# One transfer of an attention decode kernel written as 8 runs of 16 rows, and three small loads merged into others

## The chip, the cores and the metric

The kernel runs on one core of one Trainium2 chip. The metric is the device time of one execution in microseconds (us), as the median of a few runs. Beside it stands one profiled execution, whose span (first to last recorded instruction) is what the trace shows.

## The reference, cut to what matters

Two sequences (batch 2) decode one token each: a conditioned layer norm, attention over a cache of 4,096 positions in 32 heads of 128, a second conditioned layer norm and a two-layer feed-forward with Mish.

```
mod = (silu(c) @ w_mod).reshape(2, 6, 1, 512)        # sa, ca, ga, sb, cb, gb
h = layernorm(x) * (1 + ca) + sa
x = x + ga * (softmax(q(h) @ k_cache) @ v_cache) @ wo # 32 heads, 4096 positions
h = layernorm(x) * (1 + cb) + sb
x = x + gb * (mish(h @ w1 + b1) @ w2)
```

All of it is float32. The two caches hold 268 MB, the weights the rest of the 297 MB that are read; each byte is used for two tokens only.

## The kernel before, in words

All input is packed on the host into 42 loads, each one tile of SBUF with 128 rows (partitions). A head's `k` or `v` is 8,192 columns (32 KB a row). Tiles come from two pools: `one` (one buffer of 12,288 columns) and `two` (two buffers of 16,384 columns), in the rotation two, one, two. So three loads are on the chip at a time, and `used()` issues load n as soon as all that load n-3 held has been consumed. SyncE (SP) issues every load, in the order of the list that `stream()` writes, on one queue; the transfers of a load are cut at the widths that stand beside its keys. ScalarE (ACT) issues three small loads at the start on a queue of its own: the two rows of `head` (`cq`, `xq`, 8 partitions each) and `b1c` (128 partitions of 48 B).

Load 0 holds three parts of `w_mod` (`m012`) and the first two blocks of `wq`. TensorE (PE) makes the first modulation and the first `q` from it. Then for each head VectorE (DVE) multiplies `k` by `q` (L316) and sums over the head's 128 elements (L319), ACT takes the exponentials (L339), and PE multiplies them with `v` (L365), some heads behind.

The last three loads set the tail. The first holds the last block of `wo`, `m4`, and the last head's `v` in three transfers; the second `m3` and `w1` in three; the third `m5` and `w2` in five, whose last two are 512 columns each (2 KB a row, 256 KB in all). When the last `v` has been used, a chain of small steps follows on all engines: `x2`, its mean and variance (`centred`), the modulations by `m4` and `m3`, the hidden layer `w1ps` (L521), Mish, and the output `yps` (L561), which uses `w2` block by block. `busy(n)` puts matmuls on PE whose result is not used. SP at last stores `y` (L571).

Of the kernel before, what the change touches and what calls it, by code (L numbers as in the profile page):

```python
# [8 lines left out]
F32 = mybir.dt.float32  # L9
# [4 lines left out]
P = 128  # L14
WIDTHS = (384, 384, 352, 256)
CHUNKS = [(g, j) for j in range(3) for g in range(4) if WIDTHS[g] > P * j]
HEADS = 32
HC = 4
BIG = 8192
W = 2048  # L20
SIZES = {
    "k": BIG, "v": BIG, "wq": W, "wo": W, "m012": 3 * W, "m3": W, "m4": W, "m5": W,
    "w1": 4 * sum(WIDTHS), "w2": 512 * len(CHUNKS),
}
AHEAD = (14, 22)


def stream():

    behind, pieces = {}, [("k", 0)]
    for h in range(1, HEADS):
        pieces.append(("k", h))
        if h not in AHEAD:
            behind[h] = len(behind)
            pieces.append(("v", behind[h]))
    left = list(range(len(behind), HEADS))
    pieces += [("v", h) for h in left[:-1]]

    extra = {}
    for c in range(2, HEADS // HC):
        at = (pieces.index(("k", HC * c)) - 1) // 5 * 5
        extra[at] = [("wq", c), ("wo", c - 2)]
    extra[60] = [("wo", HEADS // HC - 2)]
    loads = [[([("m012", 0), ("wq", 0), ("wq", 1)], (3 * W, 2 * W))]]
    n = 0
    while n < len(pieces):
        m = 1 if n % 5 == 0 else 2
        keys = pieces[n : n + m]  # L50
        if keys[0] == ("v", left[0]) and m == 2:
            loads.append([([key], (BIG,)) for key in keys])
        else:
            keys = keys + (extra.pop(n, []) if m == 1 else [])
            loads.append([(keys, (sum(SIZES[kind] for kind, _ in keys),))])
        n += m
    assert not extra and len(loads) % 3 == 0
    last = HEADS - 1
    loads += [
        [([("wo", HEADS // HC - 1), ("m4", 0)], (2 * W,)), ([("v", last)], (BIG // 2, BIG // 4, BIG // 4))],  # L60
        [([("m3", 0), ("w1", 0)], (W, 2 * sum(WIDTHS), 2 * sum(WIDTHS)))],
        [([("m5", 0), ("w2", 0)], (W, 6 * 512, 3 * 512, 512, 512))],
    ]
    return loads, behind, left
# [3 lines left out]
def kernel(  # L68
# [1 line left out]
    tc: tile.TileContext,  # L70
    loads: list,
    head: bass.AP,
    b1c: bass.AP,
    behind: dict,
    left: list,
    out: bass.AP,
# [9 lines left out]
    nc = tc.nc  # L86
    ctx.enter_context(tc.manual_schedule())
    B = 2
    DH = 128
    D = 512  # L90
    G = D // P
    R = P // G
    TB = R // B
    H = HEADS
    NS = BIG // (B * DH)
    NJ = 3
    EPS = 1e-5
    SCALE = DH ** -0.5
    NCH = len(CHUNKS)

    const = ctx.enter_context(tc.tile_pool(name="const", bufs=1))
    work = ctx.enter_context(tc.tile_pool(name="work", bufs=2))
# [18 lines left out]
    def take(t, keys):  # L121
        lo = 0
        for kind, n in keys:
            part = t[:, lo : lo + SIZES[kind]]
            lo += SIZES[kind]
            if kind in "kv":
                (k_t if kind == "k" else v_t)[n] = part.rearrange("p (b j d) -> p b j d", b=B, d=DH)
            elif kind in ("wq", "wo"):
                (wq_t if kind == "wq" else wo_t)[n] = part.rearrange("p (k n) -> p k n", k=G)
            else:  # L130
                w_t[kind] = part.rearrange("p (k n) -> p k n", k=NCH if kind == "w2" else G)

    w_t = {}
    done = set()

    def load(n):

        t = room(n)
        lo = 0
        for keys, srcs in loads[n]:  # L140
            take(t[:, lo:], keys)
            for src in srcs:
                nc.sync.dma_start(out=t[:, lo : lo + src.shape[-1]], in_=src)  # L143
                lo += src.shape[-1]

    loaded = 0

    def used(*keys):

        nonlocal loaded  # L150
        done.update(keys)
        while loaded < len(loads) and (
            loaded < 3 or all(key in done for keys, _ in loads[loaded - 3] for key in keys)
        ):
            load(loaded)
            loaded += 1
# [1 line left out]
    used()  # L158


    cq = work.tile([P, P], F32, tag="xn", name="cq", bufs=1)
    xq = const.tile([P, P], F32, name="xq")
    for t, src in ((cq, head[0]), (xq, head[1])):
        nc.gpsimd.memset(t, 0.0)
        nc.scalar.dma_start(out=t[::TB, :], in_=src)
    bias = const.tile([P, NCH + 1], F32, name="bias")
    nc.scalar.dma_start(out=bias, in_=b1c)
    nc.scalar.preload_act_table_set("natural_log_exp_and_others")
    ident = const.tile([P, P], F32, name="ident")
    make_identity(nc, ident)  # L170
# [3 lines left out]
        out=fold, in_=ident.rearrange("p (g r) -> p r g", g=G), axis=AX.X, op=ALU.add  # L174
# [3 lines left out]
        out=mean_w, in0=fold[:, None, :].to_broadcast([P, G, R]), scalar1=1.0 / D, scalar2=None, op0=ALU.mult  # L178
# [55 lines left out]
    def modulation(name, n, t, ps=None, ks=range(G)):  # L234


        if ps is None:
            ps = wide_ps(f"modps{name}")[:, : n * P].rearrange("p (m n) -> p m n", m=n)
        for k in ks:
            for g in range(G):  # L240
                nc.tensor.matmul(  # L241
                    ps[R * g : R * (g + 1)],
                    lhsT=ct[:, k, :],
                    rhs=t[:, k, :].rearrange("p (m n) -> p m n", m=n)[:, :, P * g : P * (g + 1)],
                    start=(k == 0),
                    stop=(k == G - 1),
                )
        return ps
# [8 lines left out]
    xn = work.tile([P, P], F32, tag="xn", name="xn", bufs=1)  # L257
    xc, var, rs = centred(xq, "a")
# [1 line left out]
    nc.vector.tensor_scalar(out=xn, in0=xc, scalar1=y0, scalar2=y1, op0=ALU.mult, op1=ALU.mult)  # L260

    fps = psum.tile([P, 512], F32, tag="att2", name="fps", bufs=1)[:, : NJ * G * B]
    nc.tensor.matmul(fps, lhsT=ident, rhs=bias[:, :, None].to_broadcast([P, NJ * G, B]), start=True, stop=False, skip_group_check=True)  # L263

    ps = modulation("0", 3, w_t["m012"])
    hq = const.tile([P, P], F32, name="hq")
# [1 line left out]
    nc.vector.tensor_tensor(out=hq, in0=ps[:, 0, :], in1=hq, op=ALU.add)  # L268
    mod = {}

    def keep(m, ps):
        mod[m] = const.tile([P, P], F32, name=f"mod{m}")
        nc.scalar.copy(mod[m], ps)

    keep(2, ps[:, 2, :])
    hps = columns(hq, "hps")
    hc = const.tile([P, G, B], F32, name="hc")
    nc.vector.tensor_copy(hc, hps)  # L278
# [14 lines left out]
    def busy(n):  # L293

        for lo in range(0, n, 2):
            cols = P * min(2, n - lo)
            nc.tensor.matmul(ov[1][:, :cols], lhsT=ident, rhs=e_t[0][0].rearrange("p c m -> p (c m)")[:, :cols], start=True, stop=True)
# [130 lines left out]

    project_q(0)
    project_q(1)  # L430
    used(("m012", 0), ("wq", 0), ("wq", 1))
    for h in range(H):
        products(h)
        if h:
# [61 lines left out]
    def add_x(total):  # L496
        nc.vector.scalar_tensor_tensor(x2, xg, 1.0, xq, op0=ALU.mult, op1=ALU.add, accum_out=total)

    mps3 = modulation("3", 1, wm3, ks=(0, 1))

    def more_work():
        modulation("3", 1, wm3, mps3, (2, 3))
        busy(1)

    xc, var, rs = centred(x2, "b", add_x, more_work)
    busy(6)
    nc.vector.tensor_tensor(out=m4, in0=xc, in1=m4, op=ALU.mult)
    y0, y1 = rstd(var, rs)
    nc.scalar.activation(xc, m4, AF.Copy, scale=y0)
# [37 lines left out]

    nc.vector.tensor_scalar(out=f[:, 0], in0=hid, scalar1=30.0, scalar2=None, op0=ALU.min)
    nc.scalar.activation(f[:, 0], f[:, 0], AF.Exp)
    keep(5, gps[:, 0, :])  # L550
    busy(6)
    nc.vector.scalar_tensor_tensor(f[:, 1], f[:, 0], 2.0, f[:, 0], op0=ALU.add, op1=ALU.mult)
    nc.vector.tensor_scalar(out=f[:, 2], in0=f[:, 1], scalar1=2.0, scalar2=None, op0=ALU.add)
# [20 lines left out]
def _lay_out(np, a):  # L574


    def rows(w):

        return w.reshape(-1, P, w.shape[-1]).transpose(1, 0, 2)

    def q_rows(v):

        return v.reshape(2, 4, P).transpose(1, 0, 2).reshape(8, P)

    B, H, S, DH = a["A_k_cache"].shape
    kv = {
        kind: a[n].reshape(B, H, P, -1).transpose(1, 2, 0, 3).reshape(H, P, -1)
        for kind, n in (("k", "A_k_cache"), ("v", "A_v_cache"))
    }
    wq = rows(a["A_wq"]).reshape(P, 4, 8, 512).transpose(2, 0, 1, 3).reshape(8, P, -1)  # L590
    wo = a["A_wo"].reshape(8, 4, P, 512).transpose(0, 2, 1, 3).reshape(8, P, -1)
    wm = rows(a["w_mod"])
    w1 = rows(a["B_w1"])
    starts = np.cumsum((0,) + WIDTHS)
    b1c = np.zeros((P, 12), a["B_b1"].dtype)
    w2 = np.zeros((P, len(CHUNKS), 512), a["B_w2"].dtype)
    for n, (g, j) in enumerate(CHUNKS):
        f0 = starts[g] + P * j
        f1 = min(f0 + P, starts[g + 1])
        b1c[: f1 - f0, n] = a["B_b1"][f0:f1]  # L600
        w2[: f1 - f0, n] = a["B_w2"][f0:f1]

    pieces = {**kv, "wq": wq, "wo": wo, "m012": [wm[:, :, :1536]], "w1": [w1], "w2": [w2]}
    for n in (3, 4, 5):
        pieces[f"m{n}"] = [wm[:, :, 512 * n : 512 * (n + 1)]]
    arrays = {
        "head": np.stack([q_rows(a["c"]), q_rows(a["A_x"])]),
        "b1c": b1c,
    }
    for n, parts in enumerate(stream()[0]):  # L610
        for i, (keys, widths) in enumerate(parts):
            row = np.concatenate([pieces[kind][m].reshape(P, -1) for kind, m in keys], axis=1)
            cuts = np.split(row, np.cumsum(widths)[:-1], axis=1)
            for j, t in enumerate(cuts):
                arrays[f"load{n}_{i}_{j}"] = np.ascontiguousarray(t)
    return arrays

# [23 lines left out]
```

## Time and profile before

| what | us |
|---|---|
| median of 3 runs | 699.19 (699.03 to 699.2) |
| profiled execution, its own time | 698.83 |
| its span | 697.0 |
| DVE busy in the span | 595.8 (85%) |
| PE busy in the span | 308.2 (44%) |
| packets on SP's queue, as a share of 16 DMA engines | 98.9% |

The profiled execution is 0.36 us under the median, and 1.8 us of it lie outside the span. The busy shares are means over the whole kernel; the last 40 us have other limits than the rest.

### The profile page before, as it was taken

How to read it: one execution, taken by the hardware profiler on the slowest of the kernel's cores; microseconds unless marked ns; L12 is line 12 of the kernel's file. 1: busy time of each engine (PE TensorE's matmuls, PEld its weight loads, DVE VectorE, ACT ScalarE, POOL GpSimd, SP SyncE). 2: the span in 40 equal slices, each digit the busy share in tenths (PEclk: the TensorE clock that was granted, in tenths of full speed). 3: DMA queues.
4: the chain of work that ended last, by engine and by line, in shares of the span. 5: the costliest groups of instructions: out<-in, count | busy, mean ns of one | idle time of the engine just before them, and what ended most of it. 6: DMA issues, size and time to landing. Idle time of an engine off the chain costs nothing.

```text
span 697.0 us, 4072 instructions
## 1 busy us (share of the span) xinstructions
PE 308.2 (44%) x1692; PEld 107.0 (15%) x1692; DVE 595.8 (85%) x218; ACT 43.7 (6%) x176; POOL 4.4 (1%) x22
## 2 busy tenths in 40 slices
PE   2913343523453722843034831644043832226686
PEld 1300011100110200310011200211010300002234
DVE  3399999959999769999999789999999689999501
ACT  1100000000000000010000100000000100000001
POOL 2000000000000000000000000000000000000000
PEclk9966656776556765695665865986556975666799
DMA  9999999999999999999999999999999999999996
GB/s 383 453 429 417 427 459 411 448 429 416 454 432 425 438 425 428 448 430 433 429 444 426 432 440 417 446 432 429 444 423 440 430 425 440 429 420 432 422 422 269
DMA packets 7842, 297.48 MB, mean 427 GB/s; under 512 B 1016, under 2 KB 1040, under 8 KB 1424
## 3 DMA queue, kind: packets, MB, share of 16 engines
q1 hardware_dynamic: 7648, 297.21, 98.9%
q8 instruction: 13, 0.21, 0.1%
q10 hardware_dynamic: 176, 0.01, 0.0%
q14 instruction: 5, 0.04, 0.0%
HBM read 297.22 MB, written 0.00 MB: 426 GB/s over the span
## 4 chain that ended last, share of the span: by engine, by line
DVE 72%; DMA 24%; PE 2%; issue 1%; POOL 0%; SPq 0%; ACT 0%; DVEq 0%; POOLq 0%
DVE s L319 35%; DVE two L316 25%; DMA two<-in_load 22%; DVE one L316 10%; DMA bias<-in_b1c 2%; DVE d L326 1%; PE qps L288 1%; PE modps L241 1%; DVE m L324 1%; DVE m L337 0%; DVE pick L357 0%; SPq L143 0%; DVE pick L356 0%; PE fps L263 0%; ACT q L291 0%
## 5 line engine op out<-in xcount | busy, mean ns | idle before, releaser
L316 DVE TENSOR_TENSOR two<-two,q 128x8192 f32<-128x8192 f32 x24 | 208.5, 8687 | 37.1 <-DMA two<-in_load 37.1
L319 DVE TENSOR_REDUCE s<-two 128x64 f32<-128x8192 f32 x24 | 208.2, 8675 | 0.0
L365 PE MATMUL ov<-two,e 128*32 128x512 f32 x864 | 148.0, 847 | 134.1 <-DMA two<-in_load 81.9
L331 PE MATMUL mt<-d,ones 128*128 128x256 f32 x64 | 28.6, 536 | 130.3 <-DVE d L326 130.3
L316 DVE TENSOR_TENSOR one<-one,q 128x8192 f32<-128x8192 f32 x8 | 69.5, 8685 | 7.9 <-ACT q L291 7.9
L365 PEld LDWEIGHTS ov<-two,e 128*32 128x32 f32 x864 | 33.8, 149 | 233.4 <-issue 110.3
L319 DVE TENSOR_REDUCE s<-one 128x64 f32<-128x8192 f32 x8 | 69.4, 8676 | 0.0
L339 ACT ACTIVATE e<-s,m 128x32 f32<-128x32 f32 x64 | 20.1, 314 | 483.0 <-DVE m L337 483.0
L288 PE MATMUL qps<-one,hc 128*128 128x512 f32 x96 | 45.0, 624 | 0.0
L365 PE MATMUL ov<-one,e 128*32 128x512 f32 x160 | 28.1, 867 | 32.8 <-ACT e L339 17.1
L331 PEld LDWEIGHTS mt<-d,ones 128*128 128x128 f32 x64 | 12.0, 235 | 153.5 <-DVE d L326 108.9
L348 PE MATMUL l<-l,ones 128*128 128x8 f32 (+2 forms) x18 | 5.4, 370 | 63.4 <-ACT e L339 63.4
L288 PEld LDWEIGHTS qps<-one,hc 128*128 128x128 f32 x96 | 18.9, 201 | 24.4 <-issue 24.1
L348 PEld LDWEIGHTS l<-l,ones 128*128 128x128 f32 x18 | 4.5, 312 | 68.9 <-ACT e L339 68.5
L337 DVE TENSOR_REDUCE m<-mt 128x2 f32<-128x256 f32 x32 | 13.4, 418 | 1.4 <-PE mt L331 1.4
L326 DVE TENSOR_TENSOR d<-ident,m 128x256 f32<-128x256 f32 x32 | 13.6, 425 | 1.1
L365 PEld LDWEIGHTS ov<-one,e 128*32 128x32 f32 x160 | 6.3, 154 | 52.0 <-ACT e L339 17.9
L288 PE MATMUL qps<-two,hc 128*128 128x512 f32 x32 | 14.0, 595 | 0.3 <-DVE hc L278 0.3
L387 PE MATMUL otp<-pick,o 128*128 128x8 f32 (+2 forms) x72 | 10.0, 264 | 7.6 <-DVE m L324 4.7
L291 ACT ACTIVATE q<-qps 128x512 f32<-128x512 f32 x16 | 9.4, 594 | 52.2 <-PE qps L288 52.2
L339 ACT ACTIVATION_READ_ACCUMULATOR e<-s,m 128x1 f32 x64 | 12.0, 187 | 0.0
L387 PEld LDWEIGHTS otp<-pick,o 128*128 128x128 f32 x72 | 9.2, 200 | 14.8 <-ACT o L379 9.1
(105 smaller groups left out, 95.0 us busy)
## 6 DMA issues: line engine op xcount, KB each, us to landing
one<-in_load SPq DMA_DIRECT2D x6, 6144.0 KB, 31.8
one<-in_load SPq DMA_DIRECT2D x6, 4096.0 KB, 29.7
two<-in_load SPq DMA_DIRECT2D x2, 4096.0 KB, 24.7
two<-in_load SPq DMA_DIRECT2D x3, 2048.0 KB, 14.8
one<-in_load SPq DMA_DIRECT2D x1, 5120.0 KB
two<-in_load SPq DMA_DIRECT2D x1, 3072.0 KB
two<-in_load SPq DMA_DIRECT2D x3, 1024.0 KB, 20.7
one<-in_load SPq DMA_DIRECT2D x2, 1376.0 KB
```

The source lines that it names most:

```text
L241: nc.tensor.matmul(ps[R * g : R * (g + 1)], lhsT=ct[:, k, :], rhs=t[:, k, :].rearrange("p (m n) -> p m n", m=n)[:, :, P * g : P * (g + 1)] ...
L288: nc.tensor.matmul(ps, lhsT=hc[:, k, b : b + 1].to_broadcast([P, P]), rhs=wq_t[ch][:, k, :], start=(k == 0), stop=(k == G - 1))
L291: nc.scalar.activation(q_t[ch][:, b].rearrange("p h d -> p (h d)"), ps, AF.Copy, scale=SCALE)
L316: nc.vector.tensor_tensor(out=k_t[h], in0=k_t[h], in1=qv, op=ALU.mult)
L319: nc.vector.tensor_reduce(out=s_t[h], in_=k_t[h], axis=AX.X, op=ALU.add)
L326: nc.vector.tensor_tensor(out=d, in0=ident[:, None, :].to_broadcast([P, B, P]), in1=m_t[h][:, 0:2, None].to_broadcast([P, B, P]), op=ALU.mult,
L331: nc.tensor.matmul(mps[h], lhsT=ones, rhs=d, start=True, stop=True)
L337: nc.vector.tensor_reduce(out=m[:, 2:4], in_=mps[h], axis=AX.X, op=ALU.max, negate=True)
L339: nc.scalar.activation(e_t[i][b][:, :, M * i + 4 * b : M * i + 4 * b + 4], s_t[h][:, b].rearrange("p (c m) -> p c m", m=4), AF.Exp, bias=m ...
L348: nc.tensor.matmul(lps[n][:, x], lhsT=ones, rhs=l_t[n][:, x], start=True, stop=True)
L365: nc.tensor.matmul(ov[bank][R * g : R * (g + 1), :], lhsT=e_t[h % HC][b][:, c, :], rhs=v_t[h][:, b, 4 * c : 4 * c + 4, :].rearrange("p m d ...
L387: nc.tensor.matmul(tps[:, x], lhsT=o_t[m], rhs=pick_t[n][:, m, x], start=(m == 0), stop=(m == 3),)
```

## The change

Five things are done at once. (1) The two `head` transfers become one of 8 partitions with 1 KB each, into one tile `first` of which `cq` and `xq` are halves. (2) `b1c` is no longer a load of its own: its 12 columns stand in load 0 behind `m012`, whose transfer has 6,156 columns now; `wq` stands 48 B further on in each row. (3) `m3` and the first half of `w1` come in one transfer of 4,800 columns, where there were two of 2,048 and 2,752. (4) The transfer of the last `wo` and `m4` (4,096 columns) is cut in two: 3,584 columns as before, and the last 512 columns (`LOW`) from an array of 8 blocks of 17 rows, of which 16 rows each are read; in the words of the change, only the lower eight of the 16 DMA engines move it. (5) In the tail the modulation by `m3` is no longer made in two halves around the mean, but in one piece behind the variance, and `busy` fills the places that it left; `mod5` is kept in another tile.

```diff
--- before.py
+++ after.py
@@ -20,8 +20,9 @@
 SIZES = {
     "k": BIG, "v": BIG, "wq": W, "wo": W, "m012": 3 * W, "m3": W, "m4": W, "m5": W,
-    "w1": 4 * sum(WIDTHS), "w2": 512 * len(CHUNKS),
+    "b1": 12, "w1": 4 * sum(WIDTHS), "w2": 512 * len(CHUNKS),
 }
+LOW = 512
 AHEAD = (14, 22)
@@ -43,7 +44,7 @@
-    loads = [[([("m012", 0), ("wq", 0), ("wq", 1)], (3 * W, 2 * W))]]
+    loads = [[([("m012", 0), ("b1", 0), ("wq", 0), ("wq", 1)], (3 * W + 12, 2 * W))]]
@@ -57,8 +58,8 @@
     loads += [
-        [([("wo", HEADS // HC - 1), ("m4", 0)], (2 * W,)), ([("v", last)], (BIG // 2, BIG // 4, BIG // 4))],
-        [([("m3", 0), ("w1", 0)], (W, 2 * sum(WIDTHS), 2 * sum(WIDTHS)))],
+        [([("wo", HEADS // HC - 1), ("m4", 0)], (2 * W - LOW, LOW)), ([("v", last)], (BIG // 2, BIG // 4, BIG // 4))],
+        [([("m3", 0), ("w1", 0)], (W + 2 * sum(WIDTHS), 2 * sum(WIDTHS)))],
         [([("m5", 0), ("w2", 0)], (W, 6 * 512, 3 * 512, 512, 512))],
     ]
@@ -140,8 +140,11 @@
             for src in srcs:
-                nc.sync.dma_start(out=t[:, lo : lo + src.shape[-1]], in_=src)
-                lo += src.shape[-1]
+                if len(src.shape) == 3:
+                    src = src[:, : P // src.shape[0]]
+                n = src.shape[-1]
+                nc.sync.dma_start(out=t[:, lo : lo + n], in_=src)
+                lo += n
@@ -158,13 +161,11 @@
-    cq = work.tile([P, P], F32, tag="xn", name="cq", bufs=1)
-    xq = const.tile([P, P], F32, name="xq")
-    for t, src in ((cq, head[0]), (xq, head[1])):
-        nc.gpsimd.memset(t, 0.0)
-        nc.scalar.dma_start(out=t[::TB, :], in_=src)
-    bias = const.tile([P, NCH + 1], F32, name="bias")
-    nc.scalar.dma_start(out=bias, in_=b1c)
+    first = const.tile([P, 2 * P], F32, name="first")
+    nc.gpsimd.memset(first, 0.0)
+    nc.scalar.dma_start(out=first[::TB, :], in_=head)
+    cq = first[:, 0:P]
+    xq = first[:, P : 2 * P]
@@ -260,7 +261,7 @@
-    nc.tensor.matmul(fps, lhsT=ident, rhs=bias[:, :, None].to_broadcast([P, NJ * G, B]), start=True, stop=False, skip_group_check=True)
+    nc.tensor.matmul(fps, lhsT=ident, rhs=w_t["b1"].to_broadcast([P, NJ * G, B]), start=True, stop=False, skip_group_check=True)
@@ -496,14 +497,10 @@
-    mps3 = modulation("3", 1, wm3, ks=(0, 1))
-
-    def more_work():
-        modulation("3", 1, wm3, mps3, (2, 3))
-        busy(1)
-
-    xc, var, rs = centred(x2, "b", add_x, more_work)
-    busy(6)
+    busy(3)
+    xc, var, rs = centred(x2, "b", add_x, lambda: busy(4))
+    busy(1)
+    mps3 = modulation("3", 1, wm3)
@@ -547,7 +544,7 @@
-    keep(5, gps[:, 0, :])
+    keep(5, gps[:, 0, :], work, tag="xc", bufs=1)
@@ -600,18 +597,20 @@
     arrays = {
-        "head": np.stack([q_rows(a["c"]), q_rows(a["A_x"])]),
-        "b1c": b1c,
+        "head": np.ascontiguousarray(np.concatenate([q_rows(a["c"]), q_rows(a["A_x"])], axis=1)),
     }
...
             for j, t in enumerate(cuts):
+                if widths[j] == LOW and keys[0][0] == "wo":
+
+                    t = np.concatenate([t.reshape(8, 16, LOW), np.zeros((8, 1, LOW), t.dtype)], axis=1)
                 arrays[f"load{n}_{i}_{j}"] = np.ascontiguousarray(t)
```

SP's instructions show parts (3) and (4) at the last three loads: `two_1302` or `two_1297` is the tile with `wo`, `m4` and the last `v`, `one_` the one with `m3` and `w1`, and `two_1388` or `two_1383` the one with `m5` and `w2`. Before:

```order
L143 DMA two_1302<-in_load_0_0 128x4096
L143 DMA two_1302<-in_load_1_0 128x4096
L143 DMA two_1302<-in_load_1_1 128x2048
L143 DMA two_1302<-in_load_1_2 128x2048
L143 DMA one_1327<-in_load_0_0 128x2048
L143 DMA one_1327<-in_load_0_1 128x2752
L143 DMA one_1327<-in_load_0_2 128x2752
L143 DMA two_1388<-in_load_0_0 128x2048
L143 DMA two_1388<-in_load_0_1 128x3072
```

In the changed kernel:

```order
L146 DMA two_1297<-in_load_0_0 128x3584
L146 DMA two_1297<-in_load_0_1 128x1x512
L146 DMA two_1297<-in_load_1_0 128x4096
L146 DMA two_1297<-in_load_1_1 128x2048
L146 DMA two_1297<-in_load_1_2 128x2048
L146 DMA one_1323<-in_load_0_0 128x4800
L146 DMA one_1323<-in_load_0_1 128x2752
L146 DMA two_1383<-in_load_0_0 128x2048
L146 DMA two_1383<-in_load_0_1 128x3072
```

The transfer of 4,096 columns has become one of 3,584 and one of 512, written as `128x1x512`, and behind the three pieces of `v` one transfer of 4,800 columns stands where 2,048 and 2,752 stood. The number of transfers in the three loads is the same, and so are all columns.

PE's instructions show part (5), from the last `xps` of the attention output to the first matmuls of the hidden layer: `modps` is the modulation by `m3`, `mean_b` and `var_b` the two means in `centred`, `ov` the matmuls of `busy`, and `h2ps` the transposed input of `w1ps`. Before:

```order
L403 MATMUL xps<-two_1302,ot_168 32x128 x4
L241 MATMUL modps_1468<-one_1327,ct 32x128 x8
L204 MATMUL mean_b<-rs_b,mean_w 128x1
L241 MATMUL modps_1468<-one_1327,ct 32x128 x8
L297 MATMUL ov_105<-e_0_159,ident 128x128
L212 MATMUL var_b<-rs_b,mean_w 128x1
L297 MATMUL ov_105<-e_0_159,ident 128x256 x3
L231 MATMUL h2ps<-ident,hq 128x8
L297 MATMUL ov_105<-e_0_159,ident 128x128
L521 MATMUL w1ps<-one_1327,h2t 32x384 x2
```

In the changed kernel:

```order
L404 MATMUL xps<-two_1297,ot_163 32x128 x4
L298 MATMUL ov_100<-e_0_154,ident 128x256
L298 MATMUL ov_100<-e_0_154,ident 128x128
L205 MATMUL mean_b<-rs_b,mean_w 128x1
L298 MATMUL ov_100<-e_0_154,ident 128x256 x2
L213 MATMUL var_b<-rs_b,mean_w 128x1
L298 MATMUL ov_100<-e_0_154,ident 128x128
L242 MATMUL modps_1478<-one_1323,ct 32x128 x16
L232 MATMUL h2ps<-ident,hq 128x8
L298 MATMUL ov_100<-e_0_154,ident 128x128
L518 MATMUL w1ps<-one_1323,h2t 32x384 x2
```

The 16 matmuls of `modps` stood ahead of and behind `mean_b`; they now stand in one piece behind `var_b`, directly ahead of `h2ps`, and matmuls of `busy` stand where they were.

## Rows read from the trace of the kernel before

**Rows 1.** The page: span, DMA share in 40 slices, DMA queues.

```profile
span 697.0 us, 4072 instructions
...
DMA  9999999999999999999999999999999999999996
...
DMA packets 7842, 297.48 MB, mean 427 GB/s; under 512 B 1016, under 2 KB 1040, under 8 KB 1424
...
q1 hardware_dynamic: 7648, 297.21, 98.9%
q8 instruction: 13, 0.21, 0.1%
q10 hardware_dynamic: 176, 0.01, 0.0%
```

**Rows 2.** Timeline of the start: start us, us, engine line op, [idle before <-releaser].

```profile
2.12 34.46 SPq L143 DMA_DIRECT2D two<-in_load  x2
...
14.93 0.62 PE L263 MATMUL fps<-bias,ident 128*128 128x24 f32 x2 [3.01 <-DMA bias<-in_b1c]
...
30.02 8.69 DVE L316 TENSOR_TENSOR one<-one,q 128x8192 f32<-128x8192 f32 x1 [7.85 <-ACT q L291]
```

**Rows 3.** Stretches of the start: us, busy us by engine, PEclk, DMA share, GB/s.

```profile
30.00:40.00 10.00, 6.22 (x15) 2.47 (x13) 9.95 (x2) 1.19 (x2) 0.00 (x0) 1.00 1.00 433
40.00:50.00 10.00, 1.22 (x2) 0.50 (x2) 9.93 (x4) 0.00 (x0) 0.00 (x0) 0.57 0.97 419
```

**Rows 4.** DMA queues of 5 to 15 us: packets by size; packets, MB, share of 16 engines.

```profile
DMA packets 424, 4.49 MB, mean 449 GB/s; under 512 B 187, under 2 KB 203, under 8 KB 203
...
q10 hardware_dynamic: 176, 0.01, 1.3%
```

**Rows 5.** Chain that ended last, from 640 us: start us, us, what.

```profile
653.77 20.74 DMA two<-in_load
...
674.53 18.52 DMA two<-in_load
693.05 0.04 issue
693.09 0.47 PE yps L561 x8
```

**Rows 6.** Timeline of the tail, same columns as the second group.

```profile
677.73 0.62 PE L241 MATMUL modps<-one,ct 128*32 128x128 f32 x16
...
679.04 0.65 PE L241 MATMUL modps<-one,ct 128*32 128x128 f32 x16
...
681.43 0.35 DVE L510 SCALAR_TENSOR_TENSOR hq<-xc_b,rs_b,modps 128x128 f32<-128x128 f32 x1
...
682.55 2.77 PE L521 MATMUL w1ps<-one,h2t 128*32 128x384 f32 x32
683.66 0.97 PEld L521 LDWEIGHTS w1ps<-one,h2t 128*32 128x32 f32 x16 [0.32 <-DMA one<-in_load]
...
690.04 1.52 PE L561 MATMUL yps<-two,actt 128*32 128x128 f32 x48 [0.81 <-DMA two<-in_load]
...
691.80 1.08 PE L561 MATMUL yps<-two,actt 128*32 128x128 f32 x32 [0.25 <-DMA two<-in_load]
...
693.09 0.42 PE L561 MATMUL yps<-two,actt 128*32 128x128 f32 x8 [0.21 <-DMA two<-in_load]
```

**Rows 7.** DMA queues of 690 to 693.2 us, the slices 0.08 us each.

```profile
GB/s 230 358 205 205 282 230 230 307 230 230 282 205 179 179 307 128 154 128 128 128 128 102 102 102 102 102 102 102 102 77 51 26 0 0 0 0 0 0 0 0
DMA packets 195, 0.43 MB, mean 136 GB/s; under 512 B 28, under 2 KB 28, under 8 KB 194
...
q1 hardware_dynamic: 194, 0.42, 33.6%
q8 instruction: 1, 0.02, 2.4%
```

More of the change, by code (lines that the diff above doesn't have):

```diff
@@ L72 @@
     head: bass.AP,
-    b1c: bass.AP,
     behind: dict,
@@ L130, in take @@
             else:
-                w_t[kind] = part.rearrange("p (k n) -> p k n", k=NCH if kind == "w2" else G)
+                w_t[kind] = part.rearrange("p (k n) -> p k n", k={"b1": NCH + 1, "w2": NCH}.get(kind, G))
     w_t = {}
@@ L269, with keep @@
     mod = {}
-    def keep(m, ps):
-        mod[m] = const.tile([P, P], F32, name=f"mod{m}")
+    def keep(m, ps, pool, **kw):
+        mod[m] = pool.tile([P, P], F32, name=f"mod{m}", **kw)
         nc.scalar.copy(mod[m], ps)
-    keep(2, ps[:, 2, :])
+    keep(2, ps[:, 2, :], const)
     hps = columns(hq, "hps")
@@ L430 @@
     project_q(1)
-    used(("m012", 0), ("wq", 0), ("wq", 1))
+    used(("m012", 0), ("b1", 0), ("wq", 0), ("wq", 1))
     for h in range(H):
@@ L601, in _lay_out @@
         w2[: f1 - f0, n] = a["B_w2"][f0:f1]
-    pieces = {**kv, "wq": wq, "wo": wo, "m012": [wm[:, :, :1536]], "w1": [w1], "w2": [w2]}
+    pieces = {**kv, "wq": wq, "wo": wo, "m012": [wm[:, :, :1536]], "b1": [b1c], "w1": [w1], "w2": [w2]}
     for n in (3, 4, 5):
```

## The prediction

> **What bounds the kernel now.** I read the page first: packets on SP's queue fill 98.9% of 16 DMA engines' time, no slice of the 40 but the last is under nine tenths, and the mean is 427 GB/s [rows 1], so 26.7 GB/s for each engine. DVE is second with 85%, but it waits for transfers and not the reverse, as the stretches at the start show: from 30 to 50 us the DMA share stays at 0.97 to 1.00 while load 3 is issued only at 36.6 us (2.12 plus 34.46) [rows 2, 3]. So the queue never ran dry, and the time is the bytes of the slowest DMA engine plus what follows its last byte.
>
> Next the chain that ended last: from 653.77 us it is two transfers, 20.74 and 18.52 us, the second issued as soon as the first has landed. It lands at 693.05, and one group of `yps` follows [rows 5]. The timeline of the tail says the same from PE's side: `yps` waits for `w2` three times, 0.81, 0.25 and 0.21 us [rows 6]. Everything behind 693.05 is fixed work: 3.95 us to the span's end.
>
> Last, the queues from 690 to 693.2 us in slices of 0.08 us [rows 7], the view on which most here rests. The last transfers have 2 KB rows, and an engine that moves one packet in a slice gives 25.6 GB/s. So the row counts engines: 230 GB/s is nine at work, 128 five (691.36 to 691.68), 102 four (691.68 to 692.32), then 77, 51 and 26 are three, two and one, and at 692.56 none. All have the same share of every load, yet some end more than 2 us before others, and the last four end within 0.24 us of each other. What delays single engines is also there: 13 packets of 16 KB on an instruction queue [rows 1], one of them in this window, with 2.4% of 16 engines over 3.2 us, so 1.23 us on one engine [rows 7].
>
> **The change part by part.**
>
> The 8 runs. The transfer of 512 columns is 256 KB, 16 KB an engine, or 0.61 us at 26.7 GB/s. The upper eight lose that: -0.61 us each. The lower eight get 32 KB in 16 packets of 2 KB at 0.08 us: 1.28 us in place of 0.61, so +0.67 us. It stands 39 us ahead of the end in the queue, but since no engine is ever idle, that goes through to each one's last byte.
>
> The small loads. ACT's queue took 1.3% of 16 engines in a window of 10 us: 2.08 us in all, 0.13 us an engine [rows 4]. Left of it are eight packets of 1 KB (an estimate at 26.7 GB/s: 0.04 us each, on the lower eight; the two `head` transfers were 16 packets of 512 B before, the 203 less 187 of that row) and 384 B an engine in load 0 (0.014 us). That saves 0.08 us on a lower engine and 0.11 on an upper one. PE's wait of 3.01 us for `bias` goes too [rows 2], and DVE can begin its first head up to that much earlier than at 30.02. I cost this at nothing: DVE's start moves no transfer while the engines are full [rows 3]. If they were not, it would be worth up to 3 us.
>
> The merged `m3` and `w1`. Eight packets and one completion an engine are saved. A 2 KB packet takes 0.080 us where 26.7 GB/s would make it 0.077, so I take 0.003 us a packet, 0.03 us an engine.
>
> The tail. `modps` waited for `m3` alone and now waits for half of `w1` too. The second half of `w1` ended a wait at 683.66 [rows 6]; it has 1.41 MB, 3.3 us at 427 GB/s, so the first half lands near 680.4, and near 680.9 with the half microsecond that a late lower engine adds. The matmuls take 0.62 and 0.65 us [rows 6]: done at 682.2, where `hq` stood at 681.43. That is 0.7 to 0.8 us of delay on the chain to `yps`. It is covered: `yps` waits 0.81 us for its first block, and that block lands half a microsecond later as well, so some 1.3 us are there. Without the cover it would cost its 0.8 us.
>
> The sum for a lower engine: +0.67 - 0.08 - 0.03 = +0.56 us. For an upper one: -0.61 - 0.11 - 0.03 = -0.75. What counts is who is last. If the very last engine is a lower one, the end moves by +0.56; if a lower one is among the last four, it is at most 0.24 us before the end, and the end moves by +0.32 at least. No view names the engines. Four engines drawn from 16 are all of one given half in 8x7x6x5 of 16x15x14x13 cases, 4 in 100. Beside that stands a reading that no view prints and on which I lean only for the chance: followed packet by packet, each one's start against the end of the one before, the trace puts two of the last four engines among the eight that carried `head`. I take the middle, +0.4 us.
>
> [...]
>
> The sum is made against the profiled execution: 698.83 + 0.4 = 699.23. That one is 0.36 us under the median of the runs, so I forecast 699.6.
>
> **The rivals.**
>
> All four late engines are upper ones. Then the upper end 0.75 us earlier, near 691.8, and the lower ones, of which the last stops at 691.68 at the latest by the count, end at 692.24 with their 0.56: 0.32 us before 692.56. The median would be 698.9. For it speaks that something does delay engines in a pattern; against it the draw of 4 in 100 and the packet reading.
>
> The change doesn't do what it says: the 8 runs are spread over 16 engines all the same. Then only the savings of 0.1 to 0.15 us stay: 699.1. The `head` transfers speak against it, 8 packets each for 8 rows [rows 4].
>
> The 48 B shift. No row here shows a long transfer that stands off a multiple of 256 B. `wq` in load 0 has 8 rows of 16 KB an engine, 131 KB, 4.9 us at 26.7 GB/s, and `m012` 197 KB, 7.4 us. The lower bound is nothing. The slowest long packets in the trace are those of the instruction queue, 16 KB in 1.23 us, 13.3 GB/s [rows 1, 7]; if `wq`'s rows went at that, it would be +4.9 us, 704.5, and with `m012` +12.3. [...] It decides from a loss of 11% on the two transfers (1.4 of 12.3 us). This is the way to a slower kernel.
>
> The instruction packets fall elsewhere. PE has one matmul more, and the engine that gets a packet may be another. The engines end in steps: nine at work up to 690.9, five from 691.36, four up to 692.3 [rows 7], so one packet of 16 KB is worth about 1.3 us. One such packet more on an engine that is already last and lower: 699.6 + 1.3 = 700.9.
>
> **How the numbers follow.** Forecast (a lower engine is among the last): 0.73, with 699.5 to 699.8 as its own range. All late ones upper: 0.12. Spread over 16: 0.05. The 48 B shift: 0.04. Instruction packets elsewhere, later by one: 0.06. The range reaches from the second case, 698.9, to near the last, 700.9; with 0.5 us below for what differs between the runs and the profiled one, and 0.4 left off above where a chance of 0.06 lies, it is 698.4 to 700.5. A measurement of this kernel tells 0.2% from no change, 1.4 us: faster means under 697.8, which no case gives, and I leave 0.04 for what I have not seen; slower means over 700.6: the 48 B shift and most of the last case, 0.08 in all. Same: 0.88.
>
> **What would show it.** In the queues of the last 3 us the lower engines should end later than before and the upper earlier: the last half microsecond should hold fewer than four engines and end near 692.9, and the last landing in the chain should be near 693.4. ACT's queue falls from 176 packets to some 16, and the transfer of 512 columns brings 128 packets of 2 KB. `fps` should wait no more for `bias`, and DVE's first `k` should start 2 to 3 us earlier with no gain from it. `hq` should stand near 682.2, and `yps` should still wait for `w2` at its first block. I am wrong if the first `yps` block waits for DVE, if the first load lands over 1 us later than before, or if the last engines stop before 692.2.

## The result and the profile after

The changed kernel takes 702.77 us, the median of six runs (701.25 to 704.38). The kernel before took 699.11 us beside it (six runs, 698.9 to 699.35). The ratio is 1.0048 with a 95% interval of 1.0038 to 1.0058, so it is slower by about half a per cent, 3.7 us between the medians. The forecast was 699.6 with a range up to 700.5: it is missed on the upper side. The six executions lie 3.1 us apart, those of the kernel before here 0.45; but its 26 executions beside the first experiments lie 3.0 us apart (698.73 to 701.72), so a wide spread is not new.

The profiled execution took 701.52 us, 1.25 us under the median. The page of the changed kernel, its span and its DMA queues:

```profile
span 699.6 us, 4069 instructions
...
q1 hardware_dynamic: 7640, 297.22, 98.9%
q8 instruction: 13, 0.21, 0.1%
...
q10 hardware_dynamic: 16, 0.01, 0.0%
```

ACT's queue has 16 packets where it had 176 [rows 1], SP's queue carries the same bytes and is as full as before, and the instruction queue still has 13 packets. So nothing moved to another queue; the same queue is slower.

The chain that ended last in the changed kernel (start us, us, what):

```profile
655.76 19.10 DMA two<-in_load
...
674.88 20.94 DMA two<-in_load
695.82 0.04 issue
695.87 0.47 PE yps L558 x8
```

It has the form of [rows 5]: two transfers end to end and then `yps`. The last landing is at 695.82 and not at 693.05, and behind it lie 3.8 us (3.95 before). All of the loss, 2.77 us in this execution, is in front of the last byte. Where it arose is found with the stretches of the span, the DMA share and GB/s at the end of each row. Of the kernel before, the first 15 us of the stream, and the stretch in which the transfer of 512 columns arrives:

```profile
5.00:20.00 15.00, 6.77 (x40) 3.39 (x40) 2.30 (x11) 0.64 (x3) 0.00 (x0) 1.00 1.04 443
657.00:670.00 13.00, 11.02 (x132) 4.47 (x128) 0.29 (x1) 0.76 (x2) 0.00 (x0) 0.89 0.97 410
```

The same stretches of the changed kernel, and four slices of 1 us in the second of them:

```profile
5.00:20.00 15.00, 8.76 (x45) 4.22 (x46) 2.96 (x14) 0.91 (x4) 0.00 (x0) 1.00 0.96 409
657.00:670.00 13.00, 12.26 (x119) 4.87 (x123) 1.02 (x5) 1.08 (x5) 0.00 (x0) 0.80 0.99 360
...
661.50:662.50 1.00, 1.00 (x12) 0.19 (x4) 0.00 (x0) 0.00 (x0) 0.00 (x0) 0.59 1.07 418
662.50:663.50 1.00, 1.00 (x12) 0.24 (x8) 0.00 (x0) 0.00 (x0) 0.00 (x0) 1.00 1.01 256
663.50:664.50 1.00, 1.00 (x16) 0.35 (x12) 0.00 (x0) 0.00 (x0) 0.00 (x0) 1.00 1.10 281
664.50:665.50 1.00, 1.00 (x16) 0.25 (x12) 0.00 (x0) 0.00 (x0) 0.00 (x0) 1.00 0.92 254
```

There are two losses. In the first 15 us 34 GB/s are missing: 34 x 15 us is 0.51 MB, 1.2 us at 427 GB/s. From 657 to 670 us 50 GB/s are missing: 50 x 13 us is 0.65 MB, 1.5 us. Together that is 2.7 us of the 2.77 by which the landing of this execution moved; of the 3.7 us between the medians about 1 us is not in this trace. In the second stretch the DMA share stays near 1: the engines are not idle, their packets take longer, and 256 GB/s are 16 GB/s for each of 16 engines where 26.7 were. Whether only the runs are slow or also what the other engines carry meanwhile, this view does not tell.

The first loss is of another kind. The stretch from 6 to 10 us, of the kernel before and of the changed kernel:

```profile
6.00:10.00 4.00, 0.59 (x3) 0.53 (x3) 0.83 (x4) 0.18 (x1) 0.00 (x0) 1.00 1.02 437
6.00:10.00 4.00, 0.58 (x3) 0.52 (x3) 0.73 (x4) 0.18 (x1) 0.00 (x0) 1.00 0.78 321
```

GB/s and DMA share fall together, from 437 to 321 and from 1.02 to 0.78. So here the packets hardly take longer; the engines stand idle between them for about a fifth of the time, with transfers waiting in the queue.

The timeline of the start of the changed kernel (start us, us, engine line op, [idle before <-releaser]):

```profile
2.11 31.24 SPq L146 DMA_DIRECT2D two<-in_load  x2
...
11.95 0.62 PE L264 MATMUL fps<-two,ident 128*128 128x24 f32 x2
12.50 5.09 PE L242 MATMUL modps<-two,ct 128*32 128x384 f32 x32
...
26.79 8.69 DVE L317 TENSOR_TENSOR one<-one,q 128x8192 f32<-128x8192 f32 x1 [7.85 <-ACT q L292]
...
45.86 8.69 DVE L317 TENSOR_TENSOR two<-two,q 128x8192 f32<-128x8192 f32 x1 [0.95 <-DMA two<-in_load]
```

The wait of `fps` for `bias` [rows 2] is gone and DVE starts 3.2 us earlier, as the change says. Load 3 is issued at 33.35 us (2.11 plus 31.24) where it was 36.6. It does not help: DVE now waits 0.95 us for the second head's `k`, which comes no earlier.

The timeline of the tail:

```profile
683.38 1.08 PE L242 MATMUL modps<-one,ct 128*32 128x128 f32 x32
...
684.59 0.35 DVE L507 SCALAR_TENSOR_TENSOR hq<-xc_b,rs_b,modps 128x128 f32<-128x128 f32 x1 [0.47 <-PE modps L242]
...
692.76 1.52 PE L558 MATMUL yps<-two,actt 128*32 128x128 f32 x48 [0.37 <-DMA two<-in_load]
...
694.55 1.09 PE L558 MATMUL yps<-two,actt 128*32 128x128 f32 x32 [0.28 <-DMA two<-in_load]
...
695.87 0.43 PE L558 MATMUL yps<-two,actt 128*32 128x128 f32 x8 [0.23 <-DMA two<-in_load]
```

The three waits of `yps` for `w2` are still there, 0.37, 0.28 and 0.23 us beside 0.81, 0.25 and 0.21 [rows 6]. The tail is still bound by the transfers. `modps` stands behind the variance now, without a wait for its own transfer, and `hq` is 11.2 us ahead of the last landing where it was 11.6.

The DMA queues of the last 3.2 us up to 695.96, slices of 0.08 us:

```profile
GB/s 384 307 461 307 205 461 333 205 358 307 205 231 205 205 154 179 205 410 205 179 205 128 154 179 154 154 154 154 102 51 77 51 0 0 0 0 0 0 0 0
...
q1 hardware_dynamic: 246, 0.55, 44.7%
q8 instruction: 1, 0.02, 1.9%
```

The last packets end at 695.32, half a microsecond before the landing, as in [rows 7]. By the count of engines (25.6 GB/s each) six are at work until 0.32 us before that end, where [rows 7] had four and the prediction looked for fewer: the engines now end closer together.

### The profile page after: what moved, and what is told of

Its sections match the earlier page's. It is cut to its first block, busy times and chain, and to the rows that moved or that the text cites. A ratio compares the mean times of both kernels' runs of the same rounds, so it can differ in the third digit from the quotient of the medians.

```text
span 699.6 us, 4069 instructions
## 1 busy us (share of the span) xinstructions
PE 313.1 (45%) x1694; PEld 107.5 (15%) x1694; DVE 593.7 (85%) x218; ACT 43.4 (6%) x176; POOL 4.4 (1%) x21
## 3 DMA queue, kind: packets, MB, share of 16 engines
q1 hardware_dynamic: 7640, 297.22, 98.9%
## 4 chain that ended last, share of the span: by engine, by line
DVE 62%; DMA 31%; PE 5%; issue 1%; SPq 0%; ACT 0%; DVEq 0%; POOL 0%; POOLq 0%
DVE s L320 30%; DMA two<-in_load 27%; DVE two L317 21%; DVE one L317 9%; DMA one<-in_load 4%; PE qps L289 3%; DMA first<-in_head 1%; DVE d L327 1%; PE ov L366 1%; PE modps L242 1%; DVE m L325 1%; SPq L146 0%; DVE m L338 0%; DVE pick L358 0%; PE otp L388 0%
## 5 line engine op out<-in xcount | busy, mean ns | idle before, releaser
L366 PE MATMUL ov<-two,e 128*32 128x512 f32 x864 | 152.7, 871 | 139.3 <-DMA two<-in_load 83.7
## 6 DMA issues: line engine op xcount, KB each, us to landing
two<-in_load SPq DMA_DIRECT2D x1, 3078.0 KB, 11.2
```

Source lines behind the costliest of these rows:

```text
L366: nc.tensor.matmul(ov[bank][R * g : R * (g + 1), :], lhsT=e_t[h % HC][b][:, c, :], rhs=v_t[h][:, b, 4 * c : 4 * c + 4, :].rearrange("p m d ...
```

## The experiments

Times are medians; the kernel before gave 699.23 beside the first three and `e4_halves`, 699.03 beside `e5_runs16`, `e6_pad_plain`, `e7_quarters` and `e8_stride`, and 699.02 beside the last three. The ratios are taken over all runs and are not the quotient of the two medians. After each stand the stretches in which the changed kernel had lost: first 5 to 20 us (443 GB/s before, 409 changed), then 657 to 670 us (410 and 360).

**One cause at a time.** `e1_plain_low` takes back only the 8 runs: the 512 columns come as 128 plain rows.

```diff
             for j, t in enumerate(cuts):
-                if widths[j] == LOW and keys[0][0] == "wo":
-                    t = np.concatenate([t.reshape(8, 16, LOW), np.zeros((8, 1, LOW), t.dtype)], axis=1)
```

> The changed kernel with the 512 columns read as plain 128 rows (all 16 engines), the cut and everything else kept. Theory A (eight engines that write all 128 rows disturb all 16 engines while they do it): the stretch 662 to 667 us, where the changed kernel moved 365, 238, 272, 283 and 344 GB/s per us, is back at 420 or so, and the end comes 1.6 to 3 us earlier than in the changed kernel; what stays is the 1.2 us by which load 0 was late, so 700.2 or so. Theory B (the cut or 2 KB rows at that place are what costs): the stretch stays slow and the time stays at 702 to 703. Theory C (the doubled bytes of the lower engines are what costs, as the prediction had it): 0.3 to 0.6 us are gained, no more.

Measured: 700.63, ratio 1.0025 (1.001 to 1.004). The stretches of `e1_plain_low`:

```profile
5.00:20.00 15.00, 8.53 (x46) 4.40 (x47) 2.95 (x14) 0.91 (x4) 0.00 (x0) 1.00 0.96 408
657.00:670.00 13.00, 11.94 (x130) 5.06 (x130) 0.96 (x5) 0.82 (x3) 0.00 (x0) 0.85 0.97 405
```

The second loss is gone, the first is untouched. `e2_b1_pad` does the opposite: the 8 runs stay, and `b1` is padded from 12 to 64 columns, so that load 0's rows in HBM (the memory that the loads are read from) are 24,832 B apart and not 24,624.

```diff
-    "b1": 12, "w1": 4 * sum(WIDTHS), "w2": 512 * len(CHUNKS),
+    "b1": 64, "w1": 4 * sum(WIDTHS), "w2": 512 * len(CHUNKS),
...
-    b1c = np.zeros((P, 12), a["B_b1"].dtype)
+    b1c = np.zeros((P, 64), a["B_b1"].dtype)
```

> The changed kernel with b1 padded from 12 to 64 columns, so that a row of load 0's first transfer has 24,832 B, a multiple of 256, and wq stands 256 B further on; the 8 runs are kept. Theory A (rows that start off a multiple of 256 B make that transfer slow and give gaps between packets): the first transfer lands at 10.1 to 10.3 us on the mean engine instead of 11.3, the DMA share from 6 to 10 us is back at 1.0 from 0.75 to 0.80, and the time falls by 1.1 us to 701.6. Theory B (it is the order in which the first transfers start, or the single head transfer of 1 KB rows): the share from 6 to 10 us stays near 0.8 and the time stays.

Measured: 701.47, ratio 1.0036 (1.0019 to 1.0053). The stretches of `e2_b1_pad`:

```profile
5.00:20.00 15.00, 9.16 (x47) 4.60 (x48) 2.95 (x14) 0.91 (x4) 0.00 (x0) 1.00 1.03 445
657.00:670.00 13.00, 11.50 (x128) 4.36 (x120) 0.38 (x2) 0.75 (x2) 0.00 (x0) 0.87 0.99 359
```

Now the first loss is gone and the second untouched. `e3_runs_alone` is the kernel before with nothing but the 8 runs.

```diff
-        [([("wo", HEADS // HC - 1), ("m4", 0)], (2 * W,)), ([("v", last)], (BIG // 2, BIG // 4, BIG // 4))],
+        [([("wo", HEADS // HC - 1), ("m4", 0)], (2 * W - LOW, LOW)), ([("v", last)], (BIG // 2, BIG // 4, BIG // 4))],
...
+                if widths[j] == LOW and keys[0][0] == "wo":
+                    t = np.concatenate([t.reshape(8, 16, LOW), np.zeros((8, 1, LOW), t.dtype)], axis=1)
```

> The kernel before with the 8 runs alone: the transfer of wo and m4 cut at 3,584 columns, its last 512 as 8 runs of 16 rows; nothing else changed. Theory A (the runs disturb all engines): GB/s falls to 240 to 350 for some 5 us around 662 to 667 and the end is 1.6 to 3 us later than before, 700.7 to 702, with a spread of the runs as in the changed kernel (3 us). Theory C (only the lower engines' own bytes): no slow stretch and 699.4 to 699.7.

Measured: 700.96 (699.59 to 701.96), ratio 1.0019 (1.0008 to 1.003). The eight executions lie in two groups, three from 699.59 to 699.84, the profiled one (699.84) among them, and five from 700.67 to 701.96. The stretches of `e3_runs_alone`:

```profile
5.00:20.00 15.00, 6.49 (x40) 3.24 (x40) 2.59 (x12) 0.64 (x3) 0.00 (x0) 1.00 1.03 440
657.00:670.00 13.00, 11.18 (x128) 4.35 (x120) 0.29 (x1) 0.76 (x2) 0.00 (x0) 0.88 0.99 367
```

The runs alone make the second loss, with the tail and all other loads as they were. So the two losses are independent, and their medians add up: 1.40 us in `e1_plain_low` and 2.24 in `e2_b1_pad` are 3.64 of the 3.66. With both taken out, `e6_pad_plain` keeps the merged loads and the new tail (its edit is that of `e1_plain_low` and `e2_b1_pad` together).

> Both costs taken out: b1 padded to 64 columns and the 512 columns as plain rows on 16 engines; the merged head, m3 and w1 and the tail's new order are kept. If the 48 B shift (1.1 us) and the 8 runs (1.7 us and the spread) are all that costs, this is at 699.0 to 699.2, the kernel before or 0.1 to 0.2 us under it, with a spread of the runs of 0.3 us. If the tail's order or the merged m3 and w1 cost too, it stays above 699.6.

Measured: 699.32, ratio 1.0001 (0.9991 to 1.001), spread 0.37 us. The stretches of `e6_pad_plain`:

```profile
5.00:20.00 15.00, 9.19 (x46) 4.37 (x47) 2.95 (x14) 0.91 (x4) 0.00 (x0) 1.00 1.03 443
657.00:670.00 13.00, 12.07 (x128) 4.57 (x120) 0.41 (x2) 0.75 (x2) 0.00 (x0) 0.81 0.99 414
```

Both stretches have the speed of before. The two losses are the whole loss, and the other three parts of the change together are worth nothing that can be measured (the interval is 0.7 us wide on either side).

**What of load 0 is slow.** Padding `b1` mends three things at once: the start of the rows in HBM, the odd length of a row's packet, and the place of `wq` in SBUF. `e8_stride` (with plain `LOW`) changes the first alone: the rows lie 24,832 B apart in HBM, 24,624 B of each are read, and `wq` still stands 48 B further on in SBUF.

```diff
+                if n == 3 * W + 64:
+                    n = 3 * W + 12
+                    src = src[:, :n]
...
+                if widths[j] == 3 * W + 12:
+                    t = np.concatenate([t, np.zeros((P, 52), t.dtype)], axis=1)
```

> The changed kernel with the 512 columns as plain rows, and b1 still 12 columns, but the rows of load 0's first transfer stand 24,832 B apart in HBM (a multiple of 256), of which 24,624 B are read; wq still stands 48 B off in SBUF. Theory A (rows that start off a multiple of 256 B in HBM are slow): the transfer lands at 10.0 to 10.2 us on the mean engine, like the padded one, and the time is 699.1 to 699.3. Theory B (the odd row length, or the 48 B shift in SBUF, is what costs): it lands at 11.2 and the time is 700.6, as with plain rows and no padding.

Measured: 699.35, ratio 1.0009 (0.9991 to 1.0027). The first stretch of `e8_stride`:

```profile
5.00:20.00 15.00, 9.13 (x45) 4.29 (x46) 2.96 (x14) 0.91 (x4) 0.00 (x0) 1.00 1.03 444
...
6.00:10.00 4.00, 0.94 (x4) 0.87 (x4) 0.73 (x4) 0.18 (x1) 0.00 (x0) 1.00 1.04 446
```

Full speed, and no idle time from 6 to 10 us: the loss belongs to the HBM addresses at which the rows of the first transfer start. The odd length and the shift in SBUF cost nothing to be seen. Which addresses are good is known of distances of 24,576 and 24,832 B alone, both multiples of 256; whether a smaller step would do was not tried.

**What of the runs is slow.** `e4_halves` writes the 512 columns as two transfers of 64 rows, each 8 runs of 8 rows.

```diff
-                    t = np.concatenate([t.reshape(8, 16, LOW), np.zeros((8, 1, LOW), t.dtype)], axis=1)
...
+def PACK(np, t):
+    zero = np.zeros((8, 1, LOW), t.dtype)
+    return [np.concatenate([half.reshape(8, 8, LOW), zero], axis=1) for half in (t[:64], t[64:])]
```

> The changed kernel with the 512 columns in two transfers of 64 rows, each written as 8 runs of 8 rows: first rows 0 to 63, then rows 64 to 127; all bytes arrive. Both are moved by eight engines. [...] Theory A2 (the source layout of 8 blocks or the eight-engine form as such): both halves are slow, with the same stretch as in the changed kernel, 702 to 703. [...]

Measured: 701.63, ratio 1.0038 (1.0026 to 1.005). `e5_runs16` has 16 runs of 8 rows, meant to give all 16 engines the same bytes; no view prints what one engine moves.

```diff
-                    t = np.concatenate([t.reshape(8, 16, LOW), np.zeros((8, 1, LOW), t.dtype)], axis=1)
...
+def PACK(np, t):
+    return [np.concatenate([t.reshape(16, 8, LOW), np.zeros((16, 1, LOW), t.dtype)], axis=1)]
```

> The changed kernel with the 512 columns written as 16 runs of 8 rows (16 blocks of 9 rows in HBM) instead of 8 runs of 16, so that all 16 engines move them, 16 KB each. [...] Theory A2 (the eight-engine form, with twice the bytes on one half, is what disturbs): no slow stretch, and 700.6 as with plain rows. Theory A3 (the padded array in HBM): slow as with 8 runs.

Measured: 702.08 (701.71 to 702.23), ratio 1.004 (1.0029 to 1.0051). The second stretch of `e4_halves`:

```profile
657.00:670.00 13.00, 11.81 (x123) 4.82 (x126) 1.02 (x5) 0.97 (x4) 0.00 (x0) 0.83 0.98 359
```

The second stretch of `e5_runs16`:

```profile
657.00:670.00 13.00, 12.44 (x122) 4.87 (x126) 0.97 (x5) 0.83 (x3) 0.00 (x0) 0.79 0.98 362
```

Both stretches are as slow as with the 8 runs (359 and 362 GB/s beside 360). In `e4_halves` that is the stretch which A2 asked, with a time 0.4 us under its 702. In `e5_runs16`, where A2 asked for 700.6, 1.45 us are lost beside `e1_plain_low`; A3 fits. So nothing here points to a doubled share of eight engines as the cause: with 16 runs it is the same. `e7_quarters` writes four transfers of 32 rows, each 8 runs of 4 rows.

```diff
+def PACK(np, t):
...
+    return [np.concatenate([t[i : i + 32].reshape(8, 4, LOW), zero], axis=1) for i in (0, 32, 64, 96)]
```

> The changed kernel with the 512 columns in four transfers of 32 rows, each as 8 runs of 4 rows, so each of the lower eight engines writes 4 neighbouring rows at a time. [...] Theory A2 (any eight-engine transfer disturbs): all four are slow, and 702 to 703 stays.

Measured: 702.37, ratio 1.0038 (1.0024 to 1.0052). That is 1.74 us over `e1_plain_low`, all of the loss, and the time is the one that A2 asked. Slices of 1 us of `e7_quarters`, the same as those of the changed kernel above:

```profile
661.50:662.50 1.00, 1.00 (x12) 0.21 (x8) 0.00 (x0) 0.00 (x0) 0.00 (x0) 0.80 1.02 424
662.50:663.50 1.00, 1.00 (x16) 0.36 (x12) 0.00 (x0) 0.00 (x0) 0.00 (x0) 1.00 1.23 340
663.50:664.50 1.00, 1.00 (x16) 0.24 (x8) 0.00 (x0) 0.00 (x0) 0.00 (x0) 1.00 0.99 266
```

The fall comes about 1 us later. Followed packet by packet in the trace, which no view prints, the first two quarters (rows 0 to 63) go at 0.08 to 0.09 us a packet of 2 KB almost to their end, and the slowing sets in when the first engines reach the third. A2 had all four slow, and the first two are not. That led to the next pair: does it matter which rows are written? `e9_own_rows` and `e10_other_rows` test it. Both are `e6_pad_plain` with four transfers more, 256 KB in all, each of 32 rows in 8 runs of 4 from zeros, into columns that nothing reads. They differ in one number, `FIRST`, 0 in the first and 64 in the second: the rows written are 0 to 63, twice, or 64 to 127, twice.

```diff
+FIRST = 0
...
+                    nc.sync.dma_start(out=t[p0 : p0 + 32, spare : spare + LOW], in_=src[:, :-1])
+                    p0, spare = (p0 + 32, spare) if p0 == FIRST else (FIRST, spare + LOW)
```

> The version without either cost (b1 padded, 512 columns as plain rows), plus four extra transfers of 32 rows, each as 8 runs of 4 rows of 2 KB from padded arrays, written to columns that nothing reads, behind the 512 columns: rows 0 to 31, 32 to 63, and both once more. 256 KB in all, moved by the lower eight engines alone. [...] Theory A3 (the padded source in HBM or the short runs as such): the stretch is as slow as with the 8 runs, the mean engine loses some 1.7 us on top of the bytes, 701.5 to 702.5.

> [...] Theory A3: the same as with rows 0 to 63, whichever that is.

Measured: `e9_own_rows` 700.66, ratio 1.0015 (1.0005 to 1.0024); `e10_other_rows` 703.34, ratio 1.0047 (1.003 to 1.0065). The highest of the first (700.98) is under the lowest of the second (701.85). Of `e9_own_rows`, two slices and the stretch:

```profile
662.00:664.00 2.00, 2.00 (x24) 0.58 (x20) 0.00 (x0) 0.00 (x0) 0.00 (x0) 1.00 1.03 412
664.00:666.00 2.00, 2.00 (x28) 0.62 (x24) 0.00 (x0) 0.00 (x0) 0.00 (x0) 1.00 1.09 452
...
657.00:670.00 13.00, 11.74 (x129) 4.57 (x128) 0.63 (x3) 0.75 (x2) 0.00 (x0) 0.85 0.99 409
```

The same of `e10_other_rows`:

```profile
662.00:664.00 2.00, 2.00 (x20) 0.48 (x16) 0.00 (x0) 0.00 (x0) 0.00 (x0) 0.94 1.16 247
664.00:666.00 2.00, 2.00 (x24) 0.48 (x16) 0.00 (x0) 0.00 (x0) 0.00 (x0) 1.00 1.05 236
...
657.00:670.00 13.00, 12.56 (x128) 4.42 (x120) 0.41 (x2) 0.75 (x2) 0.00 (x0) 0.80 1.00 340
```

With the same bytes, packets and sources, writing rows 64 to 127 takes 69 GB/s over 13 us beside rows 0 to 63 (340 and 409), 0.90 MB or 2.1 us, and writing rows 0 to 63 takes next to nothing (409 beside 414 in `e6_pad_plain`). Followed packet by packet, all 256 packets of 2 KB stay under 0.1 us in `e9_own_rows`, and 191 of 256 take 0.115 us or more in `e10_other_rows`. A3, which asked for the same slow stretch in both, fails. The destination rows decide.

**The merged loads alone.** `e11_before_merged` is the kernel before with one `head` transfer and a padded `b1` in load 0 (and `mod5` in its other tile).

```diff
-    loads = [[([("m012", 0), ("wq", 0), ("wq", 1)], (3 * W, 2 * W))]]
+    loads = [[([("m012", 0), ("b1", 0), ("wq", 0), ("wq", 1)], (3 * W + 64, 2 * W))]]
...
-    for t, src in ((cq, head[0]), (xq, head[1])):
...
+    nc.scalar.dma_start(out=first[::TB, :], in_=head)
```

> The kernel before with the two head rows merged and b1, padded to 64 columns, in load 0; the tail's order, m3, w1 and the last loads as before. The prediction's term for the small loads alone: 0.08 to 0.11 us off each engine, so 698.9 to 699.1, no difference that can be measured. If DVE's earlier start were worth anything, more than 0.3 us would be gained.

Measured: 699.5, ratio 1.0009 (0.9998 to 1.0019). Its start, from the timeline of `e11_before_merged`:

```profile
2.11 31.13 SPq L142 DMA_DIRECT2D two<-in_load  x2
...
26.68 8.69 DVE L313 TENSOR_TENSOR one<-one,q 128x8192 f32<-128x8192 f32 x1 [7.85 <-ACT q L288]
```

DVE begins 3.3 us earlier than at 30.02 [rows 2], load 3 is issued 3.3 us earlier, and the time does not fall. No version here beats the kernel before.

## Why the prediction was wrong

**The bound and the place of the loss: right.** The prediction made the time out of the last byte and the work behind it. The last byte moved by 2.77 us and the work behind it by less than 0.2.

**"The 8 runs": the step that failed first.** It priced the transfer by its bytes on each engine, -0.61 us on the upper and +0.67 on the lower ones, at the 26.7 GB/s an engine that 427 GB/s over 16 engines give. Neither the price of a packet nor the rest of the stream stayed as it was. Followed packet by packet, most 2 KB packets of the runs took 0.12 to 0.16 us, where plain ones take 0.084, and the long packets beside them went at 15 to 18 GB/s. The stretch fell from 410 to 360 GB/s, 1.5 us on the mean of 16 engines, and no rival named that. `e3_runs_alone` shows that this term alone has the wrong size: +1.7 us in the median where the step had +0.4. Its lower group of executions, 0.4 to 0.6 us over the kernel before, meets the +0.4 by luck: in one of just these the stretch moved 367 GB/s and not 410, 1.3 us on the mean engine, where the step has no slowing at all. That more bytes on eight engines go through to the end fits `e9_own_rows`, where nothing is slowed: 256 KB more cost 1.34 us in the median against `e6_pad_plain`, near the 1.28 us of 32 KB on a lower engine and twice the 0.61 us of an even share. But four of its ten executions are at 699.7, only 0.4 us over, so this part of the reasoning is not settled.

What slows them is settled as far as the rows: it is neither short packets, the padded array, nor the 8 runs as such (412 to 452 GB/s in `e9_own_rows`, which has all three), but the rows in which they end (236 to 247 in `e10_other_rows`). The amount is not: in `e7_quarters` only half of the bytes go to rows 64 to 127, and the stretch is nearly as slow as with the 8 runs (364 and 360 GB/s). Why rows 64 to 127 cost that and rows 0 to 63 do not is not shown: no view here prints an engine's number.

**"The 48 B shift": the second step that failed.** The sum has no term for it, and it cost 1.2 us, little of it in the packets and most in the time between them. Followed packet by packet in `e1_plain_low` and `e8_stride`, the eight packets of an engine take 8.19 and 8.00 us, and the transfer ends on the mean engine at 11.20 and 9.97: of 1.23 us only 0.19 are in the packets, the rest is idle time of the engines with transfers waiting, which the prediction's "no engine is ever idle" left out. The loss is there with rows 24,624 B apart in HBM (408 GB/s from 5 to 20 us in `e1_plain_low`), and gone in `e8_stride`, where only their distance is another (24,832 B, 444 GB/s). The rival of that name stood on the right side with a chance of 0.04, but it looked first at `wq`, which pays nothing for its place in SBUF, and had the price as 4.9 us or more. On `m012`, 7.4 us long, 1.2 us is 16%; on the two transfers for which the prediction gave its limit of 11% it is 10% of 12.3 us, just under it. This step alone gives 700.63 (`e1_plain_low`), just above the range. One of the prediction's signs of being wrong was a first load that lands over 1 us later. Followed packet by packet, its first transfer ends 1.2 us later on the mean engine (11.25 us, 10.08 before) and 0.9 us later on the last one.

The packets themselves differ little: their median is 0.927 us in `e1_plain_low` and 0.914 in `e8_stride`, 1.4% apart.

**The small loads and the merged `m3` and `w1`: right.** They were to save about 0.1 us and do not show: `e6_pad_plain` is at 1.0001 and `e11_before_merged` at 1.0009, both intervals around 1. The 0.080 us that the prediction took for a packet of 2 KB was the width of a slice in [rows 7]; the plain packets of `e1_plain_low` took 0.084, which would double its 0.03 us and change nothing. That DVE's earlier start is worth nothing while the engines are full is shown twice, in the 0.95 us wait that DVE got in its place and in `e11_before_merged`.

**The tail: right by luck.** `hq` came 0.4 us closer to the last landing, and the cover at `yps` shrank from 0.81 to 0.37 us, where the prediction left about 0.5 (1.3 less 0.8). But `modps` did not wait for `w1`'s first half; it was late because it now stands behind the variance. The number came out, the mechanism did not.

**The other rivals.** That the 8 runs stay on eight engines is not printed by a view; the 7,640 packets on SP's queue where there were 7,648, eight fewer with as many transfers and rows, fit it. The forecast of this rival, 699.1, is far off either way. The instruction queue had 13 packets as before, but on which engine each fell is not known, so this rival is not ruled out as a part of the loss: the groups of executions lie 1 to 2 us apart, and it named 1.3. It is not needed for the two losses, which `e6_pad_plain` takes out together. Whether all late engines were upper ones was not told apart: the slowing covers it.

**What stays open.** Why the executions of one kernel lie in two groups, mostly 1 to 2 us apart. The kernel before has them too: 9 of the 73 executions beside the experiments are at 700.73 to 701.72, the rest at 699.68 or less; `e11_before_merged`, without the 8 runs, has 3 of 10 so high. In `e3_runs_alone` it is 5 of 8, in `e5_runs16` and `e6_pad_plain` all executions lie within 0.5 us, so the 8 runs may make the upper group more frequent, which is not shown. Open too is why engines stand idle between packets whose rows lie 24,624 B apart in HBM (a share of 0.78 from 6 to 10 us), why rows 64 to 127 slow the queue, and how much a given number of them costs.

## What to carry to other kernels

Where the DMA engines are the bound, price a rearranged transfer not only by its bytes: here one of 8 runs a transfer slowed the whole queue to 236 to 247 GB/s while it wrote rows 64 to 127, and left it at 412 to 452 with rows 0 to 63, so first measure it alone. When small data is put into a large load, look at the distance of the rows of the packed array in HBM: 24,624 B made 409 GB/s here, 24,576 and 24,832 made 443 and 444; other distances were not tried. An earlier start of an engine that waits for a full queue was worth nothing: DVE's 3.3 us in `e11_before_merged` left the time at a ratio of 1.0009.

## What the hardware showed

- 256 KB in 2 KB packets to rows 64 to 127 by 8 runs of 4 rows: 236 to 247 GB/s for the whole queue; to rows 0 to 63: 412 to 452 GB/s.
- 16 runs of 8 rows over all rows (`e5_runs16`): 362 GB/s from 657 to 670 us, as slow as 8 runs of 16 rows (360) and two times 8 runs of 8 (359); plain rows 405 to 414.
- Rows of 24,624 B that follow each other in HBM without padding: 409 GB/s from 5 to 20 us; the same rows 24,832 B apart: 444. The engines' busy share from 6 to 10 us is 0.78 (changed kernel) and 1.04 (`e8_stride`), so the loss is idle time between packets.
- The 48 B shift of `wq` in SBUF: no loss to be seen (444 GB/s in `e8_stride`, which keeps it, and 443 before).
